# An attention kernel on one core: V fetched four pairs ahead, idle work on TensorE before the first data, the range check spread, other banks for the last two pairs

## The chip, the cores and the metric

The kernel runs on one core of one Trainium2 chip. The metric is the device time of that core in microseconds (us), median of several runs. Before the change it is 984.85 us (4 runs, 981.81 to 985.28), of which the profiled run spans 982.0 us from its first to its last instruction.

## The reference

```python
B, H, Sq, Sk, D = 16, 32, 192, 1024, 128          # bfloat16 q, k, v
scores = jnp.einsum("bhqd,bhkd->bhqk", q, k) * D ** -0.5
out    = jnp.einsum("bhqk,bhkd->bhqd", softmax(scores), v)
```

There are 512 heads, worked on as 256 pairs. A pair moves 1 MB of K and V, 96 KB of Q and 96 KB of output.

## The kernel before

TensorE does, in step n: QK of pair n, the transposes of a K that comes later, and PV of pair n-2. ScalarE takes the exponent, VectorE copies the transposed K out of PSUM (`evac`) and normalises (`onorm`), GpSimd repacks V, and SyncE issues all loads and stores on one queue. The softmax takes no maximum; instead the row sums are checked at the end, and a general path (never taken here) would redo everything. "K4" below is K of pair 4, counted from 0.

The order of loads, on SyncE:

```python
load_k(0); load_q(0); load_k(1); load_q(1); load_v(0)
for p in range(2, R):                        # R = 4: K and Q four pairs ahead
    load_k(p); load_q(p); load_v(p - 1)
for p in range(R - 1, min(NVS, NPR)):        # NVS = 10: V3 to V9 in one burst
    load_v(p)
for n in range(NPR + 2):
    if n + R < NPR:
        load_k(n + R)                        # waits until K of pair n is transposed
        load_q(n + R)                        # waits until QK of pair n is done
    if n >= 2 and n - 2 + NVS < NPR:
        load_v(n - 2 + NVS)                  # eight pairs ahead of step n
    ...                                      # stores cut
```

TensorE's program. Its code is a straight beginning, a loop of four steps that runs 62 times, and a straight end of seven steps:

```python
tr(0, 0); tr(0, 1); tr(1, 0)
for n in range(3):
    step(n)
loops = (NPR - 5) // R                       # 62
with nc.Fori(0, loops, engines=[PE], head_slot={PE: 0}, ...):
    for n in range(R):
        step(3 + n)                          # qk, tr, half a pv; twice
for n in range(3 + R * loops, NPR + 2):      # steps 251 to 257
    step(n)
```

PV accumulates in one PSUM tensor `o_ps`; PV of a pair therefore waits until `onorm` of the pair before has read it (0.95 and 0.96 us ahead of the last two). The range check is three VectorE operations over 750 columns, all after pair 249, and three short ones at the end.

Of the kernel before, what the change touches and what calls it, by code (L numbers as in the profile page):

```python
# [394 lines left out]

HINT = False
RS_LO = 2.0 ** -40
# [4 lines left out]

def _attention_kernel(nc, q, k, v, out, NVS=10):
    B, H, SQ, D = q.shape
# [16 lines left out]
    of = out.rearrange("b h s d -> (b h) s d")  # L421

    with ExitStack() as outer:
        redo = outer.enter_context(nc.sbuf_tensor("redo", [1, 1], mybir.dt.int32))
# [4 lines left out]
        s_set = sem("f_set")  # L429
        s_kn = [sem("f_kn%d" % i) for i in range(R)]  # L430
        s_q = [sem("f_q%d" % i) for i in range(R)]
        s_v = [sem("f_v%d" % i) for i in range(NVS)]
# [13 lines left out]
        with ExitStack() as es:  # L446
# [6 lines left out]

            kn = sb("f_kn", [128, R, 2 * T * D], BF16)

# [14 lines left out]
            k_ps = ps("f_k", [128, SK], BF16)  # L470

            block = es.enter_context(nc.Block())

            @block.sync
            def _(e):
                def load_k(p):
                    if p >= R:
                        e.wait_ge(s_tr, 2 * (p - R) + 2)
                    e.dma_start(
                        kn[:, p % R, :].rearrange("m (x c) -> m x c", x=2),  # L480
                        kf[2 * p:2 * p + 2].rearrange("x (m t) d -> m x (t d)", t=T),
                    ).then_inc(s_kn[p % R], 16)

                def load_q(p):
                    if p >= R:
                        e.wait_ge(s_qk, 2 * (p - R) + 2)
                    e.dma_start_transpose(
                        qt[:, p % R, :, :],
                        qf[2 * p:2 * p + 2].rearrange("g (p j) d -> (g p) (j d)", j=3),
                    ).then_inc(s_q[p % R], 16)  # L490

                def load_v(p):
                    if p >= NVS:
                        e.wait_ge(s_pv, p - NVS + 1)
                    e.dma_start(
                        vs[:, p % NVS, :, :],
                        vf[2 * p:2 * p + 2].rearrange("x (m t) d -> m x (t d)", t=T),
                    ).then_inc(s_v[p % NVS], 16)

                def store(g):  # L500
                    so = g % NSO
                    h0 = 2 * GP * g
                    last = GP * (g + 1) == NPR
                    if last:
                        e.wait_ge(s_fin, 1)
                    else:
                        e.wait_ge(s_rc, GP * (g + 1) + 1)
                    e.dma_start(
                        of[h0:h0 + 2 * GP].rearrange("(a x) (p j) d -> (x p) a (j d)", x=2, j=3),
                        ob[:, so, :, :],  # L510
                    ).then_inc(s_st[so], 16)

                load_k(0)
                load_q(0)
                load_k(1)
                load_q(1)
                load_v(0)
                for p in range(2, R):
                    load_k(p)
                    load_q(p)  # L520
                    load_v(p - 1)
                for p in range(R - 1, min(NVS, NPR)):
                    load_v(p)
                for n in range(NPR + 2):
                    if n + R < NPR:
                        load_k(n + R)
                        load_q(n + R)
                    if n >= 2 and n - 2 + NVS < NPR:
                        load_v(n - 2 + NVS)
                    if n >= 3 and (n - 2) % GP == 0:  # L530
                        store((n - 2) // GP - 1)
                store(NPR // GP - 1)
                for so in range(min(NSO, NPR // GP)):
                    e.wait_ge(s_st[so], 16 * len(range(so, NPR // GP, NSO)))

# [18 lines left out]
            def _(pe):  # L554
# [3 lines left out]

                def tr(p, y):
                    if y == 0:  # L560
                        take(s_kn[p % R], 16)
                    if (p, y) != (0, 0):
                        take(s_ev, 1)
                    ins = None
                    for t in range(T):
                        for z in range(2):
                            c0 = (8 * y + t) * D + 64 * z
                            ins = pe.transpose(  # L568
                                k_ps[64 * z: 64 * z + 64, t * 128: t * 128 + 128],
                                kn[:, p % R, c0: c0 + 64], ident[:], tile_position=(0, 64 * z))  # L570
                    ins.then_inc(s_tr, 1)

                def qk(h):
                    p, x = divmod(h, 2)
                    if x == 0:
                        take(s_q[p % R], 16)
                        if p == NPR - 1:
                            take(s_ev, 1)
                    if h >= 2:
# [17 lines left out]
                def pv(p, lo, hi):  # L597
                    if lo == 0:
                        take(s_vp, 1)
                        if p >= NPR - 1:  # L600
                            take(s_exp, 2)
                        if p >= 1:
                            take(s_on, 1)
                    ins = None
                    for j, t in order[lo:hi]:
                        for x in range(2):
                            ins = pe.matmul(  # L607
                                o_ps[64 * x: 64 * x + 64, j * 129: j * 129 + 129],
                                pt[:, (2 * p + x) % NP, t * SQ + j * 64: t * SQ + j * 64 + 64],
# [6 lines left out]
                def step(n):  # L616
                    for x in range(2):
                        if n < NPR:
                            qk(2 * n + x)
                        if n + 1 + x < NPR:  # L620
                            tr(n + 1 + x, 1 - x)
                        if n >= 2:
                            pv(n - 2, 12 * x, 12 * x + 12)

                pe.wait_ge(s_set, 3)
                tr(0, 0)
                tr(0, 1)
                tr(1, 0)
                for n in range(3):
                    step(n)  # L630
                loops = (NPR - 5) // R
                with nc.Fori(0, loops, engines=[mybir.EngineType.PE], hint_back_edge=HINT,
                             head_slot={mybir.EngineType.PE: 0}):
# [9 lines left out]
            def _(dve):  # L643
                cnt = [0]

                def done(ins):
                    ins.then_inc(s_dv, 1)
                    cnt[0] += 1
                    dve.wait_ge(s_dv, cnt[0])

                def evac(p, y):
                    dve.wait_ge(s_tr, 2 * p + y + 1)
                    if p >= R:
                        dve.wait_ge(s_qk, 2 * (p - R) + 2)
                    dve.tensor_copy(  # L655
                        kt[:, p % R, 8 * y: 8 * y + 8, :],
                        k_ps[:].rearrange("d (t c) -> d t c", c=128),
                    ).then_inc(s_ev, 1)

                def onorm(p):  # L660
                    g, a = divmod(p, GP)
                    so = g % NSO
                    O = o_ps[:, 0:387].rearrange("p (j c) -> p j c", j=3)
                    ri = rinv[:, 3 * p: 3 * p + 3]
                    dve.wait_ge(s_pv, p + 1)
                    dve.reciprocal(ri, O[:, :, 128]).then_inc(s_rc, 1)  # L666
                    dve.wait_ge(s_rc, p + 1)
                    if a == 0 and g >= NSO:
                        dve.wait_ge(s_st[so], 16 * (g // NSO))
                    dve.tensor_tensor(  # L670
# [5 lines left out]

                def check(lo, hi, i):
                    done(dve.tensor_scalar(chk[:, lo:hi], rinv[:, lo:hi], 1.0 / RS_HI, 1.0 / RS_LO, ALU.max, ALU.min))  # L678
                    done(dve.tensor_tensor(chk[:, lo:hi], chk[:, lo:hi], rinv[:, lo:hi], ALU.not_equal))  # L679
                    done(dve.tensor_reduce(bad[:, i: i + 1], chk[:, lo:hi], mybir.AxisListType.X, ALU.max))  # L680

                early = max(NPR - 6, 1)
                evac(0, 0)
                evac(0, 1)
                evac(1, 0)
                for n in range(NPR + 2):
                    for x in range(2):
                        if n + 1 + x < NPR:
                            evac(n + 1 + x, 1 - x)
                    if n >= 2:  # L690
                        onorm(n - 2)
                        if n - 2 == early - 1:
                            check(0, 3 * early, 0)
                check(3 * early, 3 * NPR, 1)
                dve.sem_inc(s_fl, 1)  # L695
# [51 lines left out]
```

## Time and profile before

| | before |
|---|---|
| device time, median | 984.85 us |
| span of the profiled run | 982.0 us |
| first reciprocal (end of PV of pair 0) | 31.8 us |
| fifth reciprocal (pair 4) | 53.2 us |
| pair 248 | 948.1 us |
| last reciprocal (pair 255) | 972.9 us |
| one step in between | 3.667 us |

VectorE starts one reciprocal for each pair, just after PV of that pair has ended, so these starts are a good clock for the progress of TensorE.

The page of the profile gives busy tenths in 40 slices (24.6 us each), the granted clock in tenths, and groups of instructions (line, engine, operation, count; busy us and mean ns; idle time before them and who ended it):

```profile
PE   5699999999999999999999999999999999999995
PEclk9799999999999999999999999999999999999998
...
L589 PE MATMUL f_s<-f_qt,f_kt 128*64 128x192 bf16 (+2 forms) x10240 | 443.5, 231 | 4.2 <-issue 4.2
...
L568 PE MATMUL f_k<-f_ident,f_kn 128*64 128x128 bf16 x8192 | 331.3, 220 | 18.5 <-PEq L557 18.5
```

From the third slice on TensorE is full (100% busy at clock 1.00 in every stretch from 60 to 950 us), so in the middle nothing but less work on TensorE could help. What can be gained lies in the first 60 us and the last 40.

The timeline has start, duration, engine, line, operation, and in brackets the idle time of the engine before it and who ended it (a q after an engine's name means its sequencer, under which the profile lists waits for semaphores and DMA issues; PEld is TensorE's weight load). The beginning:

```profile
10.20 7.17 SPq L495 DMA_DIRECT2D f_vs<-in_v_dram  x8
...
17.42 1.23 SPq L479 DMA_DIRECT2D f_kn<-in_k_dram  x1
18.88 0.88 PE L589 MATMUL f_s<-f_qt,f_kt 128*64 128x192 bf16 x20
...
29.34 0.82 PEld L568 LDWEIGHTS f_k<-f_ident,f_kn 128*64 128x64 bf16 x15 [9.79 <-issue]
```

```profile
29.37 1.07 PE L568 MATMUL f_k<-f_ident,f_kn 128*64 128x128 bf16 x16 [9.60 <-PEq L557]
...
43.66 0.58 PE L589 MATMUL f_s<-f_qt,f_kt 128*64 128x192 bf16 x11
48.48 0.85 PE L589 MATMUL f_s<-f_qt,f_kt 128*64 128x192 bf16 x9 [4.24 <-issue]
```

Eight V loads were issued from 10.2 us on, before K4 at 17.4. TensorE then stood still for 9.6 us, until K4 had come. The second pause, 4.24 us at 44 us, is of another kind: it is in the middle of a group of 20 QK matmuls (11 ran, 9 were left) and its releaser is "issue", which means that the profile shows no semaphore that it waited for. In the stretch 45 to 47 us one packet of the instruction queue (packets, MB, share of the engines' time) passed:

```profile
q8 instruction: 1, 0.02, 3.5%
```

The end. VectorE does the whole check in one go, TensorE's next transposes wait for its copy, and the last PV groups stand apart by the normalisation:

```profile
952.44 0.85 DVE L678 TENSOR_SCALAR f_chk<-f_rinv 128x750 f32<-128x750 f32 x1
...
954.30 0.94 DVE L680 TENSOR_REDUCE f_bad<-f_chk 128x1 bf16<-128x750 f32 x1
955.27 0.69 DVE L655 COPY f_kt<-f_k 128x1024 bf16<-128x1024 bf16 x1
956.11 0.64 PE L568 MATMUL f_k<-f_ident,f_kn 128*64 128x128 bf16 x16 [1.87 <-PEq L557]
```

```profile
968.67 1.60 PE L607 MATMUL f_o<-f_vp,f_pt 128*64 128x129 bf16 x48 [0.95 <-PEq L557]
...
971.23 1.60 PE L607 MATMUL f_o<-f_vp,f_pt 128*64 128x129 bf16 x48 [0.96 <-PEq L557]
```

### The profile page before, as it was taken

The page shows a single profiled execution, that of the slowest core. Times are in us where ns is not written, and L with a number is a line of the kernel's source. Part 1 is how long each engine was busy: PE and PEld are TensorE (multiplying, and loading weights), DVE is VectorE, ACT ScalarE, POOL GpSimd, SP SyncE. Part 2 cuts the span into 40 slices and gives each one's busy share as a digit, 9 for nine tenths or more (in the row PEclk, how much of TensorE's full clock was granted, in tenths as well). Part 3 has the DMA queues.
Part 4 walks back from the last instruction along what each step waited for, and adds up shares of the span by engine and source line. Part 5 has one row for each costly group of instructions (what it writes and reads, how often), then busy time and mean ns, then how long its engine had stood idle before and what let it go on. Part 6 is the DMA issues. An engine that isn't in the chain of part 4 may idle for free. (4 is left out here: it accounts for less than half of the span.)

```text
span 982.0 us, 67627 instructions
## 1 busy us (share of the span) xinstructions
PE 948.1 (97%) x30722; PEld 945.6 (96%) x30722; DVE 546.1 (56%) x1031; ACT 743.6 (76%) x513; POOL 267.7 (27%) x263
## 2 busy tenths in 40 slices
PE   5699999999999999999999999999999999999995
PEld 4699999999999999999999999999999999999995
DVE  2355555555556555555555555655555555565562
ACT  4377777777777777777777777777777777777773
POOL 2122222222222222222222222222222222222220
PEclk9799999999999999999999999999999999999998
DMA  9999999999999999999999999999999999999971
GB/s 296 256 259 349 351 347 325 354 329 353 329 348 343 332 342 341 346 328 342 351 326 344 334 350 320 361 340 301 367 349 335 350 316 347 358 336 335 347 235 38
DMA packets 279602, 319.35 MB, mean 325 GB/s; under 512 B 115712, under 2 KB 148480, under 8 KB 279552
## 3 DMA queue, kind: packets, MB, share of 16 engines
q1 hardware_dynamic: 279552, 318.84, 102.5%
q14 instruction: 37, 0.30, 0.1%
q8 instruction: 13, 0.21, 0.1%
HBM read 268.44 MB, written 25.17 MB: 299 GB/s over the span
## 5 line engine op out<-in xcount | busy, mean ns | idle before, releaser
L706 ACT ACTIVATE f_pt<-f_s 128x1536 bf16<-128x1536 f32 x512 | 742.4, 1450 | 224.1 <-PE f_s L589 223.9
L655 DVE COPY f_kt<-f_k 128x1024 bf16<-128x1024 bf16 x512 | 354.0, 691 | 408.6 <-PE f_k L568 408.6
L607 PE MATMUL f_o<-f_vp,f_pt 128*64 128x129 bf16 x12288 | 458.7, 221 | 2.2 <-PEq L557 2.2
L548 POOL COPY f_vp<-f_vs 128x1024 uint32<-128x1024 uint32 x256 | 266.8, 1042 | 694.0 <-PE f_o L607 678.9
L589 PE MATMUL f_s<-f_qt,f_kt 128*64 128x192 bf16 (+2 forms) x10240 | 443.5, 231 | 4.2 <-issue 4.2
L607 PEld LDWEIGHTS f_o<-f_vp,f_pt 128*64 128x64 bf16 x12288 | 394.9, 110 | 2.7 <-issue 2.7
L589 PEld LDWEIGHTS f_s<-f_qt,f_kt 128*64 128x64 bf16 x10240 | 359.8, 111 | 4.5 <-issue 4.5
L568 PE MATMUL f_k<-f_ident,f_kn 128*64 128x128 bf16 x8192 | 331.3, 220 | 18.5 <-PEq L557 18.5
L568 PEld LDWEIGHTS f_k<-f_ident,f_kn 128*64 128x64 bf16 x8192 | 288.3, 111 | 20.0 <-issue 19.8
L670 DVE TENSOR_TENSOR f_ob<-f_o,f_rinv 128x384 bf16<-128x384 f32 x256 | 142.7, 557 | 8.9
L666 DVE RECIPROCAL f_rinv<-f_o 128x3 f32<-128x3 f32 x256 | 46.2, 181 | 10.6 <-PE f_o L607 8.0
L706 ACT ACT_TABLE_LOAD x1 | 1.3, 1283 | 0.8 <-PEq L732 0.8
L639 PEld LDWEIGHTS f_o<-f_bad,f_ones 128*1 128x1 bf16 x1 | 0.1, 79 | 1.6 <-DVEq L695 1.6
L639 PE MATMUL f_o<-f_bad,f_ones 128*1 128x1 bf16 x1 | 0.2, 164 | 1.4 <-DVEq L695 1.4
L679 DVE TENSOR_TENSOR f_chk<-f_chk,f_rinv 128x750 f32<-128x750 f32 (+1 forms) x2 | 1.1, 560 | 0.1
L680 DVE TENSOR_REDUCE f_bad<-f_chk 128x1 bf16<-128x750 f32 (+1 forms) x2 | 1.1, 555 | 0.1
L678 DVE TENSOR_SCALAR f_chk<-f_rinv 128x750 f32<-128x750 f32 (+1 forms) x2 | 1.0, 508 | 0.0
L697 DVE CAST redo<-f_o 1x1 int32<-1x1 f32 x1 | 0.1, 147 | 0.3 <-PE f_o L640 0.3
L540 POOL TENSOR_SCALAR_AFFINE_SELECT f_ident<-f_ones 128x128 bf16<-128x128 bf16 x1 | 0.3, 292 | 0.1
L538 POOL MEMSET f_ones<- 128x128 bf16 x1 | 0.2, 204 | 0.3 <-POOLq L732 0.3
L543 POOL MEMSET f_vp<- 128x128 bf16 x1 | 0.2, 211 | 0.0
L732 POOL MEMSET const-float32-0.0<- 128x1 f32 x1 | 0.1, 98 | 0.3 <-issue 0.3
(5 smaller groups left out, 0.5 us busy)
## 6 DMA issues: line engine op xcount, KB each, us to landing
f_kn<-in_k_dram SPq DMA_DIRECT2D x256, 512.0 KB, 5.9
f_vs<-in_v_dram SPq DMA_DIRECT2D x256, 512.0 KB, 5.1
out_dram<-f_ob SPq DMA_DIRECT2D x64, 384.0 KB, 5.0
f_qt<-in_q_dram SPq DMA_TRANSPOSE x256, 4.9
```

Of the source, the lines that this page charges most:

```text
L548: gp.tensor_copy(vp[:, p % R, :, 0:D].bitcast(U32), vs[:, p % NVS, :, :].rearrange("p x (t d) -> p (x t) d", d=D).bitcast(U32),).then_inc( ...
L568: ins = pe.transpose(k_ps[64 * z: 64 * z + 64, t * 128: t * 128 + 128], kn[:, p % R, c0: c0 + 64], ident[:], tile_position=(0, 64 * z))
L589: ins = pe.matmul(S[64 * w: 64 * w + 64, c0: c0 + (j1 - j0) * 64], kt[:, p % R, 8 * x + t, 64 * w: 64 * w + 64], mv, start=True, stop=True ...
L607: ins = pe.matmul(o_ps[64 * x: 64 * x + 64, j * 129: j * 129 + 129], pt[:, (2 * p + x) % NP, t * SQ + j * 64: t * SQ + j * 64 + 64], vp[:, ...
L639: pe.matmul(o_ps[0:1, 0:1], ones[:, 0:1], bad[:, 0:1], start=True, stop=False)
L655: dve.tensor_copy(kt[:, p % R, 8 * y: 8 * y + 8, :], k_ps[:].rearrange("d (t c) -> d t c", c=128),).then_inc(s_ev, 1)
L666: dve.reciprocal(ri, O[:, :, 128]).then_inc(s_rc, 1)
L670: dve.tensor_tensor(ob[:, so, a, :].rearrange("p (j d) -> p j d", j=3), O[:, :, 0:128], ri.unsqueeze(2).to_broadcast([128, 3, D]), ALU.mul ...
L678: done(dve.tensor_scalar(chk[:, lo:hi], rinv[:, lo:hi], 1.0 / RS_HI, 1.0 / RS_LO, ALU.max, ALU.min))
L679: done(dve.tensor_tensor(chk[:, lo:hi], chk[:, lo:hi], rinv[:, lo:hi], ALU.not_equal))
L680: done(dve.tensor_reduce(bad[:, i: i + 1], chk[:, lo:hi], mybir.AxisListType.X, ALU.max))
L706: act.activation(pt[:, h % NP, :], s_ps[h % 2][:], ACT_FN.Exp, scale=scale).then_inc(s_exp, 1)
```

## The change

V is fetched four pairs ahead like K, which is meant to take the burst away from in front of K4. The first K comes in two halves, one transpose group less stands before the first QK, and TensorE multiplies ones while it waits for data, which is meant to have its clock up when they come (no_warm, below, takes this out: the full clock then came at 10.8 us, against 5.8 in the profile of the change). The check is spread over three pairs. The last two pairs put PV into banks that are free by then, and the last store is smaller.

```diff
-def _attention_kernel(nc, q, k, v, out, NVS=10):
+def _attention_kernel(nc, q, k, v, out, NVS=6):
...
+    stores = [(p, GP) for p in range(0, NPR - GP, GP)] + [(NPR - GP, GP - 1), (NPR - 1, 1)]
+    EARLY = NPR - 8
...
+            def o_of(p):
+                if p == NPR - 1:
+                    return s_ps[0][:, 0:512]
+                if p == NPR - 2:
+                    return k_ps[:].bitcast(F32)
+                return o_ps[:]
...
-                for p in range(2, R):
-                    load_k(p)
-                    load_q(p)
-                    load_v(p - 1)
-                for p in range(R - 1, min(NVS, NPR)):
-                    load_v(p)
+                load_k(2)
+                load_q(2)
+                load_v(1)
+                load_k(3)
+                load_q(3)
+                load_v(2)
+                load_v(3)
                 for n in range(NPR + 2):
                     if n + R < NPR:
                         load_k(n + R)
                         load_q(n + R)
-                    if n >= 2 and n - 2 + NVS < NPR:
-                        load_v(n - 2 + NVS)
+                        load_v(n + R)
...
-                        if p >= 1:
+                        if 1 <= p <= NPR - 3:
                             take(s_on, 1)
...
                     for x in range(2):
-                        if n + 1 + x < NPR:
-                            tr(n + 1 + x, 1 - x)
+                        h = 2 * n + x
+                        if h + 2 < NH:
+                            tr(h + 2)
...
+                pe.wait_ge(s_set, 1)
+                for _i in range(8):
+                    pe.matmul(o_ps[:], ones[:], ones[:].unsqueeze(1).to_broadcast([128, 4, 128]),
+                              start=True, stop=True)
                 pe.wait_ge(s_set, 3)
-                tr(0, 0)
-                tr(0, 1)
-                tr(1, 0)
+                tr(0)
+                tr(1)
...
-                        if n - 2 == early - 1:
-                            check(0, 3 * early, 0)
+                        if 0 <= n - 2 - EARLY < 3:
+                            check(0, 3 * EARLY, 0, n - 2 - EARLY)
```

## The prediction

> **What bounds the kernel now.** In steady state TensorE: the table of stretches shows PE 100% busy in every stretch from 100 to 950 us at clock 1.00, and in the timeline the reciprocals of successive pairs start 3.667 us apart. Nothing is late inside a step: K and V land 5.9 and 5.1 us (medians) after issue and are needed two to three steps later. The change can gain only at the two ends.

> **Where the ends lose (timeline of before).**
> - 19.8 to 29.4 us: TensorE idle. Eight V loads (pairs 2 to 9) are issued from 10.2 us, ahead of K of pair 4, which is issued at 17.4 and lands at 29.1 (a backlogged 512 KB transfer lands every 1.33 us). The clock is halved from 23.8 to 34.0.
> - 44.0 to 48.5: TensorE stops inside a QK group, waiting for nothing that the profile names; a 16 KB packet of the instruction queue starts at 45.8. [...] I read this as the loop's last block coming late; with the cold clock it costs 5.7 us.
> - 954.2 to 956.1: 1.9 us; the range check (0.85+0.94+0.94 us) holds up VectorE's K copy.
> - 967.7 to 971.2: twice 0.95 us; PV waits for the normalisation of the pair before.

> **The change, costed.**
> 1. V four pairs ahead: only V2 and V3 stand ahead of K4. With the landing rhythm of before (K3 at 15.0) K4 lands at about 20, 9 earlier. The steady state is unchanged: V is still issued well before POOL needs it.
> 2. First K in halves, one transpose group less ahead of the first QK, idle matmuls [...]: first QK at about 7 instead of 9.3. But the third and fourth K (11.8, 15.0) then bound TensorE, so most of it is not seen: first reciprocal at about 18.5.
> 3. K4 then leaves about 1.5 us of stall; the second reciprocal comes at about 24.7 instead of 36.6: 12 us gained.
> 4. Instruction fetch is not removed: TensorE enters the loop earlier, and the loop's four blocks are fetched while the DMA queue is full. In before a fetch started 0.6 to 5.6 us after the block ahead of it was entered; 2.5 us more pass until it runs, against 3.8 us per block. I estimate 3 to 4 us of stalls, against 5.7: 2 us gained.
> 5. Check spread: 0.9 us a step nearly fits VectorE's idle time; 1.8 us gained.
> 6. PV of the last two pairs in other banks: 1.9 us; smaller last store: 0.4.

> Sum 18 to 20 us, all on the critical path: 985 - 20 = 965.

> **Range and chances.** 961.5 to 970. Faster by over 2% 0.45 (the border is about 965), within 0.54, slower 0.01.

> **What would show it.** No idle stretch at 20 to 29 us; first reciprocal at 18 to 19, second at 24 to 26; interval still 3.667; no TensorE wait over 0.5 us near the check; the last PV groups back to back; one or two TensorE pauses of 1 to 4 us between 18 and 45 us that no semaphore ends, each near a 16 KB instruction packet.

> **What would make it wrong.** Instruction fetches in time (961), or later with the clock halved (over 970); K of pairs 4 to 6 slower than 1.33 us per transfer; an interval off 3.667, which costs 2.5 us per 0.01.

## The result, and the profile after

The changed kernel takes 979.17 us (median of 4, 977.56 to 979.6); its ratio to before is 0.9946 (95% interval 0.9923 to 0.9969). A ratio is the mean time of one kernel's fast runs over that of the other's of the same rounds, so not quite the ratio of the medians quoted. The prediction said 965 and at least 961.5, at most 970: it was wrong, the gain is a quarter to a third of what was forecast.

| | before | predicted | after |
|---|---|---|---|
| first reciprocal | 31.8 | 18.5 | 20.2 |
| second | 36.6 | 24.7 | 30.9 |
| fifth | 53.2 | about 38 | 46.8 |
| pair 248 | 948.1 | about 933 | 942.4 |
| pair 253 | 967.75 | about 951 | 964.67 |
| last | 972.9 | about 954 | 967.7 |
| span | 982.0 | about 963 | 975.8 |

("About": worked out from the terms of the prediction, 1.5 us of waiting for K4, 3.5 us of late instructions and 3.667 us a step.) Some 11.6 us were gained up to the first reciprocal, 5.2 of them were gone at the fifth, and the end of the kernel, where 4 us were to be gained, gave nothing on balance.

The page after, the same lines:

```profile
PE   5899999999999999999999999999999999999996
PEclk9899999999999999999999999999999999999999
...
L609 PE MATMUL f_s<-f_qt,f_kt 128*64 128x192 bf16 (+2 forms) x10240 | 443.3, 231 | 10.9 <-issue 6.4
...
L588 PE MATMUL f_k<-f_ident,f_kn 128*64 128x128 bf16 x8192 | 329.2, 219 | 6.2 <-PEq L574 4.8
```

The idle time before QK (first group) has grown from 4.2 to 10.9 us: 6.4 of it is put down to "issue", the other 4.5 is one wait at the loop's first instruction. That before the transposes, most of which is waiting for K, has gone from 18.5 to 6.2. The timeline of the beginning:

```profile
10.83 0.98 SPq L493 DMA_DIRECT2D f_kn<-in_k_dram  x1
...
20.20 0.18 DVE L691 RECIPROCAL f_rinv<-f_o 128x3 f32<-128x3 f32 x1
...
24.69 1.49 PE L609 MATMUL f_s<-f_qt,f_kt 128*64 128x192 bf16 x20 [4.52 <-PEq L574]
...
30.91 0.18 DVE L691 RECIPROCAL f_rinv<-f_o 128x3 f32<-128x3 f32 x1
...
38.58 0.64 PE L609 MATMUL f_s<-f_qt,f_kt 128*64 128x64 bf16 x13 [3.08 <-issue]
...
43.29 0.52 PE L609 MATMUL f_s<-f_qt,f_kt 128*64 128x192 bf16 x9 [0.72 <-issue]
```

K4 is issued at 10.8, seven us earlier, and the 9.6 us stall is gone. In its place TensorE stops for 4.52 us at the loop's first instruction, then 3.08 and 0.72 us in the middle of QK groups; a smaller one of 0.51 is not shown. The sum is 8.8 us. The line of the first pause names the sequencer (PEq), but the data that this QK needs had long been there: Q3 landed at 17.1 us and the exponent that frees its scores ended at 16.6. A QK group takes 1.5 us instead of 0.86 from 24.7 on: the granted clock was 0.50 from 22.9 to 29.7 us. In the stretch of the first pause one instruction packet passed, among a full data queue:

```profile
q1 hardware_dynamic: 1503, 1.52, 119.3%
q8 instruction: 1, 0.02, 1.4%
```

The end of the changed kernel:

```profile
942.88 0.64 PE L588 MATMUL f_k<-f_ident,f_kn 128*64 128x128 bf16 x16
943.13 0.85 DVE L707 TENSOR_SCALAR f_chk<-f_rinv 128x744 f32<-128x744 f32 x1
...
946.92 1.23 DVE L709 TENSOR_TENSOR f_chk<-f_chk,f_rinv 128x744 f32<-128x744 f32 x1
948.86 0.27 PE L609 MATMUL f_s<-f_qt,f_kt 128*64 128x192 bf16 x2 [2.08 <-issue]
...
953.01 0.92 DVE L711 TENSOR_REDUCE f_bad<-f_chk 128x1 bf16<-128x744 f32 x1
954.31 0.63 PE L588 MATMUL f_k<-f_ident,f_kn 128*64 128x128 bf16 x15 [1.33 <-issue]
```

```profile
964.44 1.59 PE L628 MATMUL f_k<-f_vp,f_pt 128*64 128x129 bf16 x48
965.85 1.85 PE L628 MATMUL f_s<-f_vp,f_pt 128*64 128x129 bf16 x48
```

Each part of the check now holds TensorE up little, and the last PV groups follow each other. But there are two new pauses, 2.08 and 1.33 us, in the middle of a QK and of a transpose group, again with no semaphore.

**The theory (A).** My reading is that these pauses are TensorE's own instructions coming late. What the traces show: packets of 16 KB pass on the instruction queue, five between 18 and 48 us in the change. In the loop of 994 instructions the pauses fall at its start and at the 256th, 512th and 768th instruction, in its first round only. I call the 256 instructions from one such border to the next a block, so the loop is four blocks; that one packet brings one block is part of the reading. No such packet is seen in the change from 48 to 946 us, while the loop makes its other rounds. (Thirty packets of 8 KB on another instruction queue pass in that time, and TensorE has no pause over 0.25 us then.) I placed every packet of the loop and of the end, in 12 traces (101 packets; all traces but those of hold and head160; packets that began after the last PV group left out), against the matmuls. A pause ended 1.2 to 1.9 us after the packet had ended (a packet takes about 1.1 us). And the packet began later where more data transfers were in flight:

| data transfers in flight when it began | packets | us after TensorE had entered the block ahead, median (range) |
|---|---|---|
| 0 or 1 | 50 | 1.6 (0.3 to 4.3) |
| 2 or 3 | 27 | 3.6 (0.3 to 5.5) |
| 4 or more | 24 | 4.5 (0.6 to 5.6) |

A block runs for 3.8 us, and about 2.5 us pass from the packet's start to the end of the pause; from these two I estimate that only a packet that begins within about 1.3 us is in time. When TensorE asks for a block is not recorded; that I count from entering the block ahead is my choice, not something that a trace shows. In some of these blocks TensorE ran at half the clock (0.50 in the first stretch below) or stood still, which stretches the times; but counted in matmuls that TensorE had begun of the block's 124 or so, the order is the same (medians 52, 99 and 124). The table is a correlation with wide ranges, and the experiments have to show the cause.

Three stretches of the changed kernel, each from entering a block to the start of the packet that is needed next (A:B, length, then busy us with counts of PE, weight loads, VectorE, ScalarE and GpSimd, then clock, DMA share and GB/s). TensorE worked nearly all of the time and the data queue was busy:

```profile
24.70:28.90 4.20, 4.20 (x73) 4.20 (x75) 0.69 (x1) 1.45 (x1) 0.78 (x1) 0.50 0.86 287
31.50:36.00 4.50, 3.96 (x124) 3.78 (x124) 2.22 (x5) 2.90 (x2) 1.14 (x2) 1.00 0.96 258
942.70:946.60 3.90, 3.90 (x130) 3.77 (x124) 3.00 (x6) 2.94 (x3) 1.16 (x2) 1.00 1.06 321
```

### The profile page after: what moved, and what is told of

Same layout as the page of the kernel before. It is cut to its first block, busy times and chain, and to the rows that moved or that the text cites. A ratio compares the mean times of both kernels' runs of the same rounds, so it can differ in the third digit from the quotient of the medians.

```text
span 975.8 us, 67645 instructions
## 1 busy us (share of the span) xinstructions
PE 949.3 (97%) x30730; PEld 943.4 (97%) x30730; DVE 546.5 (56%) x1031; ACT 743.8 (76%) x513; POOL 267.5 (27%) x263
## 5 line engine op out<-in xcount | busy, mean ns | idle before, releaser
L609 PE MATMUL f_s<-f_qt,f_kt 128*64 128x192 bf16 (+2 forms) x10240 | 443.3, 231 | 10.9 <-issue 6.4
L609 PEld LDWEIGHTS f_s<-f_qt,f_kt 128*64 128x64 bf16 x10240 | 359.2, 110 | 11.9 <-issue 11.8
L650 PE MATMUL f_o<-f_ones 128*128 128x512 bf16 x8 | 3.6, 631 | 1.1 <-POOL f_ones L555 1.1
```

Source lines behind the costliest of these rows:

```text
L609: ins = pe.matmul(S[64 * w: 64 * w + 64, c0: c0 + (j1 - j0) * 64], kt[:, p % R, 8 * x + t, 64 * w: 64 * w + 64], mv, start=True, stop=True ...
L650: pe.matmul(o_ps[:], ones[:], ones[:].unsqueeze(1).to_broadcast([128, 4, 128]), start=True, stop=True)
```

## The experiments

Twelve runs were made, two of them repeats (tail_loop2 of loop2_vlate, after_again of the change), all with correct results; each ratio is to the kernel before on the same chip, which took 982.6 to 983.1 us there. A pause is idle time of TensorE as its timeline shows it. Each run has one profile. The start varies between profiles: the change, its repeat, and tail_loop, vdeep and no_warm (the change without the idle matmuls), which differ from it little or not at all there, have the fifth reciprocal between 46.5 and 48.5 us; a difference of one or two us at that point is within this spread.

### The V schedule alone: v4_only

Before, with only the order of V loads of the change and its ring of 6.

```diff
-                for p in range(R - 1, min(NVS, NPR)):
-                    load_v(p)
+                load_v(2)
+                load_v(3)
...
-                    if n >= 2 and n - 2 + NVS < NPR:
-                        load_v(n - 2 + NVS)
+                        load_v(n + R)        # with NVS = 6
```

> Before with the V schedule of the change alone (ring of 6, four pairs ahead); checks, banks, stores, first K and loop as in before. Theory A (the 12 us that the changed kernel still loses before its fifth reciprocal, 46.8 us instead of an unstalled 34.9, and its new pauses at 946.8 and 952.8 are late 16 KB instruction blocks of TensorE that queue behind data transfers): K of pair 4 lands at about 21 instead of 29, the fifth reciprocal comes at 46 to 48 instead of 53.2, but V loads now run to about 950 us and delay the instruction blocks of the epilogue, so 1 to 3 us are given back at the end: 979 to 982 us against 984.8. Rival B (the end of the changed kernel suffers from the spread check on VectorE or from the new banks, not from fetches): nothing is given back here, 978 us, and no TensorE pause without a semaphore after 900 us.

Measured: 981.7 us, ratio 0.9984 (0.9970 to 0.9997). The fifth reciprocal came at 48.5 instead of 53.2, a little later than expected. From pair 248 to 253 it took 21.1 us against 19.7 before. TensorE paused 3.92 us at the loop's entry, 3.28 us at 36 us, and, near the end, 1.54 us for the check and 1.03 us with no semaphore, which B had excluded. The time lies in the range of A, but the gain is 1.5 us where I had thought of 3 to 6; the chip's own before was 2 us faster than the one that I had reckoned with.

### Everything but the V schedule: v10_only

The changed kernel with the burst of V loads and the ring of 10 put back.

```diff
-                load_v(2)
-                load_v(3)
+                load_v(2)
+                for p in range(R - 1, NVS):
+                    load_v(p)
...
-                        load_v(n + R)
+                    if n >= 2 and n - 2 + NVS < NPR:
+                        load_v(n - 2 + NVS)
```

> The changed kernel with the V schedule of before put back (ring of 10, burst of eight V loads at the start); everything else of the change stays. Theory A: the stall on K of pair 4 is back (10 us), but V loads end near 930 us, the epilogue's instruction blocks come in time, and the spread check, the other banks and the smaller last store give 4 to 5 us at the end: 979.5 to 981.5 us, no pause over 0.5 us without a semaphore between 935 and 965. Rival B: the pauses of 2.1 and 1.3 us near 947 and 953 are here too and the end gains under 1 us: 984 us.

Measured: 980.9 us, ratio 0.9984 (0.9971 to 0.9998). The time is in A's range, but against this chip's before it is a gain of 2 us, not 4 to 5. A pause of 0.99 us at 950.7 stayed, where A said none over 0.5: a half miss. It is half of the change's 2.08 us, and the second one fell from 1.33 to 0.22 us. So the pauses do depend on the V schedule, against B; but fewer V loads at the end did not do away with them. The two halves of the change gain 0.16% each (give or take 0.14) and 0.54% together: nothing shows that one takes back what the other gains.

### The end's code taken from the loop: tail_loop

```diff
-                loops = (NPR - 5) // R
+                loops = (NPR - 4) // R
```

> The changed kernel with the TensorE loop run 63 times instead of 62, so that steps 251 to 254 come from the resident loop body and not from fresh code; the same matmuls in the same order. Theory A: the two pauses and the slow third group (2.1 + 1.3 + 0.3 us) are gone, 975 to 976 us against 979.2 for the change. Rival B: same time as the change, 979, the pauses stay.

Measured: 974.28 us, ratio 0.9911 (0.9896 to 0.9927); the profiled run is the lowest of its four. A had said 975 to 976, B 979; the chip's own before was again 2 us faster than the one reckoned with. Steps 251 to 254 are one more round of the loop here, a single 16 KB packet passed from 935 to 962 us (four in the change), and the pauses are gone; the timeline of TensorE over the steps concerned has only a wait of 0.31 us for VectorE's copy:

```profile
948.50 0.64 PE L588 MATMUL f_k<-f_ident,f_kn 128*64 128x128 bf16 x16 [0.31 <-PEq L574]
```

From pair 248 to 253 it took 18.7 us instead of 22.2. The matmuls, their order and the data are those of the change; only where the instructions stand differs. This shows for the end that the pauses go with the place of the instructions, as A says, and B (the check, the banks) falls. What makes them long it does not say; that is for the next two runs.

When this kernel left the loop, the loads had ended, and the next packet began 0.9 us after its block was entered. The stretch (DMA share 0.10):

```profile
957.60:958.60 1.00, 0.71 (x23) 0.53 (x20) 0.56 (x1) 0.63 (x2) 0.00 (x0) 1.00 0.10 30
```

### More or less V traffic at the end: vdeep and vlate

vdeep starts like the change and then gains four pairs of lead, one at each of steps 30, 40, 50 and 60, so V loads end earlier. vlate fetches V two pairs ahead, so they end later.

```diff
 # vdeep, with NVS = 10
-                        load_v(n + R)
+                    while nv < min(NPR, n + R + 1 + min(4, max(0, (n - 20) // 10))):
+                        load_v(nv)
+                        nv += 1
```

```diff
 # vlate
-                load_v(2)
-                load_v(3)
...
-                        load_v(n + R)
+                    if n + R - 2 < NPR:
+                        load_v(n + R - 2)
```

> The changed kernel with a V ring of 10 that starts four pairs ahead and gains one pair of lead at each of steps 30, 40, 50 and 60, so V loads end about 15 us earlier. Theory A: with fewer transfers at the end the epilogue's blocks come earlier, 1 to 3.5 us less than the change: 975.5 to 978. Rival B: 979. If tail_loop gains and this does not, fetches are late for a reason other than V traffic.

> The changed kernel with V issued two pairs ahead instead of four, so no V stands ahead of K of pair 4 except V0 and V1. K of pair 4 should land at about 18.5 instead of 21.2. Theory A: the loop's first block comes at most 1 us earlier, and pauses of 2 to 4 us remain; the fifth reciprocal 44 to 47 us, the end as in the change or worse by up to 1 us: 977 to 980. Rival C (K of pair 4 behind V2 and V3 sets the start): the fifth reciprocal 3 us earlier, 976.

Measured: vdeep 975.25 us, ratio 0.9923 (0.9909 to 0.9936). vlate 979.0 us, ratio 0.9965 (0.9953 to 0.9978). TensorE's code is the same in both and in the change. The first two pauses after the loop, in vdeep and in vlate:

```profile
948.20 0.27 PE L612 MATMUL f_s<-f_qt,f_kt 128*64 128x192 bf16 x2 [0.98 <-issue]
952.54 0.63 PE L591 MATMUL f_k<-f_ident,f_kn 128*64 128x128 bf16 x15 [0.22 <-issue]
```

```profile
947.87 0.27 PE L608 MATMUL f_s<-f_qt,f_kt 128*64 128x192 bf16 x2 [2.99 <-issue]
955.79 0.63 PE L587 MATMUL f_k<-f_ident,f_kn 128*64 128x128 bf16 x15 [3.80 <-issue]
```

Together 1.2 us with V eight pairs ahead, 3.4 us in the change (four), 6.8 us with V two ahead. The later the V loads end, the longer the pauses, with the same TensorE code: this shows that V traffic lengthens them. Two things belong beside it. In vlate the end lost more than A had allowed: from pair 248 to 253 it took 26.9 us against 22.2 in the change, where A had said at most 1 us worse. And v4_only, with V four ahead but the end's code of before, had only one pause over 0.3 us without a semaphore there, 1.03 us; its first packet began 1.7 us after its block was entered with five transfers in flight. So the number of transfers in flight does not fix each single delay. For the beginning the fifth reciprocal of vlate came at 45.5, in A's range (44 to 47) and not 3 us earlier as C said, and the pauses summed to 9.2 us, about what they are in the change.

### Where the loop begins: loop2

The loop is entered at step 2 instead of 3, so less code stands before it and TensorE comes to it earlier (it goes on from the wait at the loop's entry at 18.0 us, at 24.7 in the change); it runs up to step 253. VectorE adds one count so that the first PV looks like the others.

```diff
-                        if 1 <= p <= NPR - 3:
+                        if p <= NPR - 3:
...
-                for n in range(3):
+                for n in range(2):
                     step(n)
-                loops = (NPR - 5) // R
+                loops = (NPR - 4) // R
...
-                        step(3 + n)
+                        step(2 + n)
...
+                dve.sem_inc(s_on, 1)
                 evac(0)
```

> The changed kernel with the TensorE loop taken from step 2 to 253 (63 times) instead of 3 to 250 (62 times); to make step 2 like the others, VectorE gives one count ahead for the first PV. Same matmuls in the same order, only the places of the code differ: fewer blocks before the loop, all asked for earlier. Theory A (the first five pairs lose 12 us to late instruction blocks and the cold clock that follows): the pauses of 4.5 and 3.1 us at 20 and 35.5 us shrink below 2 us each, the fifth reciprocal comes at 37 to 41 instead of 46.8, the end loses nothing; 968 to 973 us where the change has 979 and tail_loop 974 (ratio to before 0.984 to 0.990). Rival C (those pauses are data arriving late or a cold clock of other origin): the fifth reciprocal stays at 46 to 47, the ratio is that of tail_loop, 0.991.

Measured: 972.96 us, ratio 0.9901 (0.9886 to 0.9915). The total is as A said, but not for A's reason: the fifth reciprocal came at 45.0, not at 37 to 41, and the end did the rest, as in tail_loop. The pauses have only moved:

```profile
17.96 1.49 PE L609 MATMUL f_s<-f_qt,f_kt 128*64 128x192 bf16 x20 [3.69 <-PEq L574]
25.21 0.78 PE L609 MATMUL f_s<-f_qt,f_kt 128*64 128x192 bf16 x17 [0.68 <-issue]
32.25 0.64 PE L609 MATMUL f_s<-f_qt,f_kt 128*64 128x64 bf16 x13 [3.08 <-issue]
37.78 0.52 PE L609 MATMUL f_s<-f_qt,f_kt 128*64 128x192 bf16 x9 [1.54 <-issue]
```

They sum to 9.0 us, against 8.8 in the change. Coming to the loop earlier did not shorten them; 4 to 7 transfers were in flight as the first three of these packets began. This was my second error about the same thing. The fifth reciprocal is 1.8 us earlier all the same, hardly more than the spread between profiles; perhaps the pauses now fall partly where TensorE would wait for K anyway; that was not tested by itself.

### Both: loop2_vlate, and again beside head160

> loop2 and vlate together. Theory A: once the blocks come early, data bounds the start, and K of pair 4 two transfers (2.7 us) earlier now counts: 1 to 3 us less than loop2, 967 to 971. Rival C: as vlate alone.

> loop2_vlate with the loop placed at slot 160 of a 256-instruction block instead of slot 0: it should begin inside the block that is already there, and its second block is needed about half a step later. Theory A: the wait at the loop's entry near 15 to 18 us goes or shrinks by 1 to 2 us; up to three later pauses of 1 to 3 us remain; 967 to 970 us, 0 to 3 us less than loop2_vlate (ratio 0.984 to 0.9875). If the loop lands in the next block instead, 970 to 972.

> loop2_vlate a second time, beside head160 on the same chip, to compare the two: 970 us, ratio 0.986 to 0.989.

head160 is loop2_vlate with `head_slot={PE: 160}` instead of 0; tail_loop2 is loop2_vlate unaltered.

Measured: loop2_vlate 970.29 us, ratio 0.9874 (0.9860 to 0.9888), and the second time 971.06 us, 0.9877 (0.9861 to 0.9894). That is the fastest version found, and it beats both kernels. Its fifth reciprocal came at 42.5 us (42.9 the second time), clear of the spread; TensorE's pauses with no semaphore at the start are fewer:

```profile
21.55 0.78 PE L608 MATMUL f_s<-f_qt,f_kt 128*64 128x192 bf16 x17 [1.89 <-issue]
28.59 1.07 PE L608 MATMUL f_s<-f_qt,f_kt 128*64 128x64 bf16 x13 [3.08 <-issue]
35.27 0.52 PE L608 MATMUL f_s<-f_qt,f_kt 128*64 128x192 bf16 x9 [1.37 <-issue]
```

The fewer V transfers ahead of K4, which alone (vlate) gave 1.3 us at the fifth reciprocal, gave 2.5 here beside loop2. Why they add up so is not shown.

head160 took 971.0 us, ratio 0.9877: no gain. The time is that of the second outcome that I had named. One packet more than in loop2_vlate passed before the loop was complete (six, not five), but 994 instructions from slot 160 on reach into five stretches of 256 where they reach into four from slot 0, so this does not tell into which block the loop fell. Its pauses tell something else. They are no longer in QK but in PV:

```profile
21.72 1.07 PE L627 MATMUL f_o<-f_vp,f_pt 128*64 128x129 bf16 x15 [4.34 <-issue]
33.24 0.42 PE L627 MATMUL f_o<-f_vp,f_pt 128*64 128x129 bf16 x7 [1.59 <-issue]
```

With two smaller ones between and after (0.56 and 0.39 us) they come after 96, 352, 608 and 864 instructions of the loop: each is 160 short of 256, 512, 768 and 1024, so these are the block borders again, counted from slot 160. The work and its order are those of loop2_vlate; only the place of the code was moved, and the pauses moved with the block borders. So at the start too the pauses go with the place of the code, and not with the data.

### The start with an empty queue: hold

```diff
                     if n + R < NPR:
+                        if n < 4:
+                            e.wait_ge(s_qk, 2 * (n + R) - 1)
                         load_k(n + R)
```

> The changed kernel, slower on purpose: the loads of pairs 4 to 7 are held until the QK of the pair just ahead has begun, so the data queue is empty while TensorE asks for the blocks of the loop. Theory A (an instruction block starts 3 to 5 us after it is asked for because it queues behind data): the blocks asked for between 25 and 50 us start within 1.5 us, and every TensorE pause after the loop's entry is ended by the K semaphore (3 to 4 us for each of pairs 4 to 7); pauses that no semaphore ends, 0.5 + 3.1 + 0.7 us in the change, stay under 0.5 us each. Rival D (blocks are slow by themselves, whatever the queue holds): the pauses without a semaphore stay, on top of the K waits. Time 980 to 990.

Measured: 989.0 us (one look, state unknown). The wait at the loop's entry fell from 4.52 to 1.42 us, and the next packet began 0.45 us after that, with no data transfer in flight. Then come four waits for K (the first is shown, 4.06 us), and one pause without a semaphore, at 40.8:

```profile
21.86 0.86 PE L611 MATMUL f_s<-f_qt,f_kt 128*64 128x192 bf16 x20 [1.42 <-PEq L576]
26.78 1.06 PE L590 MATMUL f_k<-f_ident,f_kn 128*64 128x128 bf16 x16 [4.06 <-PEq L576]
...
40.80 0.64 PE L611 MATMUL f_s<-f_qt,f_kt 128*64 128x64 bf16 x13 [1.12 <-issue]
```

Of the 0.5, 3.1 and 0.7 us in the change's loop one pause of 1.12 us is left, more than the 0.5 that A allowed. Three packets also began more than 6 us after the block ahead was entered (6.5 and 6.2 us with one transfer in flight, 8.7 with six), because TensorE itself stood still for K in that block; this also gave the packets more time. A had said within 1.5 us. So the time since entering the block ahead does not by itself say when the next packet begins (8.7 us is over twice the 3.8 of a block); what matters may be how far TensorE has come in it, which no run tests by itself. The run still points to A, but it cannot tell A from D as cleanly as I had meant: the cure for the pauses and the waits for K come together.

### Without the idle matmuls: no_warm

```diff
-                pe.wait_ge(s_set, 1)
-                for _i in range(8):
-                    pe.matmul(o_ps[:], ones[:], ones[:].unsqueeze(1).to_broadcast([128, 4, 128]),
-                              start=True, stop=True)
```

> The changed kernel without the eight idle matmuls on ones. My prediction said that K of pairs 2 and 3 bounds the start, so the earlier clock is not seen: first reciprocal within 1 us of the change's 20.2, time within 1 us of 979. If the warm clock matters the first reciprocal comes 2 us later or more and the time is 981 or more.

Measured: 978.76 us, ratio 0.9958 (0.9946 to 0.9971); the first reciprocal at 19.2. The idle matmuls gain nothing that these runs can see. In the profile of the change the full clock came at 5.8 us (the transpose group at 4.6 us took 1.06 us, that at 6.5 took 0.64); without them it came at 10.8, but from 10.9 us on the change stood waiting for K2 and then for K3 (1.43 and 1.85 us), so what the clock gave was waited away. In the change's second profile (below) the full clock came only at 10.4 us with the idle matmuls, so they do not bring it early every time.

### The change a second time: after_again

> The changed kernel unaltered, a second profile, to see whether its pauses are the same from run to run. If they are late instruction blocks behind a data queue whose phase repeats: four pauses between 19 and 44 us that sum to 8 to 11 us, and two near 947 and 953 that sum to 2.5 to 4.5 us; ratio 0.993 to 0.997. If the first profile was an accident: sums that differ by more than half.

Measured: 978.02 us, ratio 0.9943 (0.9925 to 0.9960). Four pauses from 20.7 us on of 5.64, 0.74, 2.26 and 1.54 us sum to 10.2 (a further one of 2.20 us comes ahead of the loop, at 15.6); those near 948 and 954 are 1.80 and 1.31 us. The single pauses vary more than the sums (8.8 and 10.2 us at the start, 3.4 and 3.1 at the end). The fifth reciprocal came at 48.5, 1.7 us later than the first time.

## Why the prediction was wrong

- **What bounds the kernel** was right: the interval in the middle is 3.667 us before and 3.671 after, and only the ends moved.
- **Point 1 was right.** K4 landed at 21.2 us, predicted about 20 (29.1 before), and the 9.6 us stall went. The 1.5 us of waiting for K4 of point 3 never showed: K4 landed while TensorE stood at the loop's entry, until 24.7.
- **Point 2 was right in kind.** K2 and K3 bound the start of the profiled run and no_warm shows that the idle matmuls are not seen. The first reciprocal came at 20.2 instead of 18.5, where K3 landed at 16.7 us instead of 15.0. Cost: 1.7 us. In the second profile K3 landed at 14.3 and the first reciprocal still came at 20.8, after the pause of 2.20 us without a semaphore; so an earlier K3 alone would not have given 18.5.
- **Point 4 is the step that failed**: "I estimate 3 to 4 us of stalls, against 5.7: 2 us gained." The delay was named and its size was wrong. In the change the four pauses at the start took 8.8 us, and what is left, about 3, goes mostly to the clock that halved during the first of them (granted 0.50 from 22.9 to 29.7 us; 5 us of work at half the clock, worth 2.5): from the first to the fifth reciprocal it took 26.6 us, where four steps are 14.7 and I had reckoned with 19.7. The error was in how I drew the delays from the trace of before. There the burst of V had first stopped TensorE for 9.6 us, and SyncE, waiting for TensorE, let the queue run down; so the packets of the loop's next two blocks began in time (0.9 and 0.8 us after the block ahead was entered; four and three transfers were in flight by count, but the queue moved only 140 GB/s from 31.8 to 33.4 us and 159 from 36 to 40) and the packet ahead of the loop's entry (22.1 to 23.2 us) passed while TensorE waited for K4 until 29.4. I mixed such delays with others, 0.6 to 5.6, and took them as valid for a queue that the change keeps full. With four or more transfers in flight the median is 4.5 us. That the full queue is what made the pauses at the start longer is the reading that fits; no run isolates it there. Cost: 6.9 us.
- **The end was left out of point 4.** V four ahead means that V loads are issued later (the last at 946.3 us, at 937.3 before), so the first two packets for the last seven steps, at 946.6 and 951.9 us, began before the last V had landed (952.6). I had said "the steady state is unchanged" and not asked what else the later V loads would meet. Two pauses of 2.1 and 1.3 us; tail_loop shows that they go with the place of the code, and the row vdeep, change, vlate (1.2, 3.4, 6.8 us) that V traffic lengthens them. Cost: 3.4 us, and 0.3 for a third block.
- **Point 5** was a little too high. Where no such pause disturbs it (tail_loop), the three steps with a part of the check lose 0.8 us together, against 2.1 before in one: 1.25 us gained, not 1.8.
- **Point 6 was right**: from pair 253 to 255 it took 5.1 us before and 3.1 after (1.9 predicted as gain); the last store gave 1.0 instead of 0.4.

The errors sum to 13 us of the 14 that the time was missed by: 1.7 at the first reciprocal, 6.9 up to the fifth, 0.8 in the middle, 4.3 from pair 248 to 253, less 0.7 at the very end.

What stays open: when exactly TensorE asks for a block, so how much of a delay is waiting in the queue, is not in the trace; for the start, head160 shows that the pauses sit at block borders, but no run removed them without adding a wait for data, so that the data queue makes those packets late is argued from the table; and the table above has packets that began at once with four or more transfers in flight.

## What to carry to other kernels

A stall that the trace shows may be hiding another, and its idle time may be what lets some background transfer (here TensorE's instruction packets, two of which began 0.9 and 0.8 us after the block ahead was entered, as the queue ran down in before) come in time; take delays for the time after the change only from stretches in which the queue is as full as the change will make it. When a prefetch is moved, ask what runs at its new end as well as at its old beginning. Here the straight code after the loop came with two pauses of 2.1 and 1.3 us, and the same steps as one more round of the loop with none without a semaphore, by a one-line edit worth 0.35%; where a loop can take one more round, that is worth a try.
